# Block-sparse attention followed by a gated MLP: pair 6's transposes and the norm's pow moved ahead in their queues, three pairs' splits in other slots

## The chip, the cores and the metric

The kernel runs on one core of one Trainium2 chip. The metric is the device time of one execution in microseconds (us), the median of several runs. A core has five engines that run at once and wait for each other through semaphores: TensorE (PE, matrix products and transposes), VectorE (DVE), ScalarE (ACT), GpSimd (POOL) and SyncE (SP, which here issues nearly all DMAs). Every engine executes its own instructions strictly in program order, so an instruction that waits holds up all that stands behind it on its engine.

## The reference

Inputs are q, k, v of shape 4 x 8 x 768 x 64 (batch, head, position, dimension), and the weights of a gated MLP.

```python
scores = scale * np.matmul(q, k.transpose(0, 1, 3, 2))
scores = np.where(mask, scores, -1e9)      # mask by blocks of 32: window, edges, 3 sampled blocks
attn = softmax(scores)
x = np.matmul(attn, v)                     # heads side by side: 4 x 768 x 512
h = np.maximum(x @ w_in, 0.0)
u, v = h[..., :512], h[..., 512:]
v_n = (v - mean(v)) / np.sqrt(var(v) + 1e-06)
v_s = np.einsum('ts,bsd->btd', w_spatial, v_n) + b_spatial[None, :, None]
out = (u * v_s) @ w_out
```

## The kernel before

**Pairs.** Two heads make a pair p. There are 16 pairs, four to a batch element. For each head the kernel computes the scores by `qk_exp` (L361 on PE: two matmuls of 384 columns; L365 on ACT: the exponential), then the product with v by `av` (L377, six matmuls of 65 columns) and the division by the row sums by `norm` (L442 and L443 on DVE, writing `xn`). The first four pairs use versions for half of the columns: `qk_exp_half` (L396, L400), `av_half` (L412, L423, L424) and `xtr_half` (L433 on PE, L434 on DVE), which transposes `xn` into `xt`.

**How q and k get in.** `load(p)` issues three loads on SP (L110: q, k, v). `prepare(p)` casts k, q and v to bf16 on POOL (L140, L140, L143). `tr_dma(p, ...)` issues two DMA transposes on SP (L344, into `tt_k` and `tt_q`), each of which waits for its cast. `split_pair(p, "k")` and `split_pair(p, "q")` each issue two DVE copies (L350), one per head, from `tt_k` or `tt_q` into the operands `kt` and `qt` of the score matmuls. The first score matmul of a pair needs the first k copy and the first q copy.

**The order.** All instructions are issued in a hand-written order of slots; each slot holds one score step (a `qk_exp` or `qk_exp_half`), one AV step and one or two MLP steps. Slots are numbered g. The first loop has slots 0 to 47 (pairs 0 to 3); the second has 12 slots for each pair p from 4 on, g = 12p + s with s from 0 to 11. Within that loop p = NG is pair 4, and p = NP - 3 is pair 13. While pair p is computed, pair p + 1 is split, pair p + 2 is prepared and transposed, and pair p + 3 is loaded. `change` is true at pairs 8 and 12, where a new batch element begins.

**The MLP.** `moe_units(b)` returns a list of steps, one PE matmul of 512 columns each (L520), and these are popped slot by slot. A product into v goes through `v_post` (L533, L536, L537 on DVE: relu and statistics `mv`). After every third one, POOL computes `rstd` from the variance (L540 adds, L542 is the pow). `normalize` (L547 on DVE) needs `rstd` and writes `vn`, which the spatial products read (matmuls `vn,w_spt`); their results go through L586 on DVE to `gn` and by DMA transpose (L590) to `gt`, and the last products (`w_out_t,gt`) are stored from `osb` (L608, L610, L611). MLP products alternate between two PSUM banks, `moe0` and `moe1`; the third product from a given one reuses its bank. `xtr(p)` transposes `xn` by DMA (L466 on SP). `load_weights(2)` and `cast_weights(2)` bring in w_out (L175 on SP, L183 on POOL), as they do the other weights earlier.

Of the kernel before, what the change touches and what calls it, by code (L numbers as in the profile page):

```python
# [26 lines left out]
def kernel(  # L27
# [29 lines left out]
    NG = H // 2  # L57
    NP = B * NG
# [27 lines left out]
    def dram(src, b, h0, nh):  # L86
        return src[b, h0:h0 + nh].rearrange("h (p c) d -> p h (c d)", c=NCH)
# [13 lines left out]
    def st_tile(p, nm):  # L101
        if (nm, p) in st:
            return st[nm, p]
        st[nm, p] = work.tile([128, 2, NCH * D], FP32, tag=f"st_{nm}", bufs=2, name=f"st_{nm}")
        return st[nm, p]

    def load(p, names="qkv", eng=nc.sync):
        b, g = divmod(p, NG)
        for nm in names:
            eng.dma_start(out=st_tile(p, nm), in_=dram(dict(q=q, k=k, v=v)[nm], b, 2 * g, 2))  # L110
# [19 lines left out]
    def nat_tile(p, nm):  # L130
        nat[nm, p] = work.tile([128, NCH, 2, D], BF16, tag=f"nat_{nm}", bufs=2,
                               name=f"nat_{nm}")

    def cast_qk(p, nm, hs, eng):
        src = st[nm, p][:, hs].rearrange("p h (c d) -> p h c d", d=D)
        dst = nat[nm, p].rearrange("p c h d -> p h c d")[:, hs]
        if eng is nc.scalar:
            nc.scalar.activation(out=dst, in_=src, func=AF.Copy)
        else:
            eng.tensor_copy(out=dst, in_=src)  # L140

    def cast_v(p):
        nc.gpsimd.tensor_copy(  # L143
            out=vv[p % NG][:, :, :, 0:D],
            in_=st.pop(("v", p)).rearrange("p h (c d) -> p h c d", d=D))

    def prepare(p, names="kqv"):
        for nm in names:
            if nm == "v":
                cast_v(p)  # L150
            else:
                nat_tile(p, nm)
                cast_qk(p, nm, slice(0, 2), nc.gpsimd)
# [26 lines left out]
    def cast_weights(n):  # L180
        for _ in range(n):
            t, dst = w_staged.popleft()
            nc.gpsimd.tensor_copy(out=dst, in_=t)  # L183
# [26 lines left out]
    def keep_warm(n):  # L210
        for _ in range(n):
            nc.tensor.matmul(out=wps[:, 0:128], lhsT=warm, rhs=warm, start=True, stop=True)  # L212
# [51 lines left out]
    def qt_mask(h0, h1, grp, eng=nc.vector):  # L264
        cols = slice(grp * HALF, (grp + 1) * HALF)
        eng.tensor_copy(out=qt_all[D:KR, h0:h1, cols],
                              in_=qt_all[D:KR, 0:1, cols].to_broadcast([NB, h1 - h0, HALF]))
# [17 lines left out]
    def bank(shape, dtype):  # L285
        moe_bank[0] = 1 - moe_bank[0]
        return psum.tile(shape, dtype, tag=f"moe{moe_bank[0]}", bufs=1, name="ps_moe")
# [40 lines left out]
    def mask_product(hf, ps, copy):  # L328
        mq = ps[0:NB, 0:HALF]
        nc.tensor.matmul(out=mq, lhsT=bm, rhs=ind[:, hf * HALF:(hf + 1) * HALF],  # L330
                         start=True, stop=True)
        copy(qt[0][D:KR, hf * HALF:(hf + 1) * HALF], mq)
# [14 lines left out]
    def split_pair(p, nm):  # L347
        src = tt.pop((nm, p)).rearrange("x c n -> x (c n)")
        for h in range(2):
            nc.vector.tensor_copy(out=(qt if nm == "q" else kt)[(2 * p + h) % H][0:D, :],  # L350
                                  in_=src[h * D:(h + 1) * D, :])
# [34 lines left out]
    def qk_exp_half(g):  # L386
        gh, i = divmod(g, NCH // 2)
        grp, j = divmod(gh, H)
        if g % NCH == 0:
            t = work.tile([128, NCH, S], BF16, tag="a_all", bufs=3, name="a_all")  # L390
            t = t.rearrange("p c s -> p (c s)").rearrange("p (u c s) -> p u c s", u=2, c=NCH)
            a_ref["half", gh], a_ref["half", gh + 1] = t[:, 0], t[:, 1]
        ps = psum.tile([128, 1024], FP32, tag="sc", bufs=2)
        for u in range(2):
            ci = 2 * i + u
            nc.tensor.matmul(out=ps[:, u * 512:u * 512 + HALF],  # L396
                             lhsT=kt[j][:, ci * 128:(ci + 1) * 128],
                             rhs=qt[j][:, grp * HALF:(grp + 1) * HALF],
                             start=True, stop=True)
        nc.scalar.activation(out=a_ref["half", gh][:, 2 * i:2 * i + 2, :],  # L400
                             in_=ps.rearrange("p (b c) -> p b c", b=2)[:, :, 0:HALF],
                             func=AF.Exp, scale=0.125)
# [223 lines left out]
    def cast_q_pair(p, half):  # L626
        cast_q(p, half, slice(0, 2), nc.gpsimd)
# [44 lines left out]
    for g in range(N0):  # L672
        qk_exp_half(g)
        if g < 6:
            keep_warm(2)
        if g == 12:
            mask_product(1, bank([128, 512], FP32), dve_copy)
        if g == 0:
            qt_mask(1, 2, 0)
        if g == 1:  # L680
            tr_k_head(1, 0, NCH)
            cast_qk(1, "k", slice(0, 1), nc.vector)
            qt_mask(2, 4, 0)
        for p, third in tr_slots.get(g, ()):
            tr_pair(p, "k", third)
        if g in q_slots:
            tr_q_pair(*q_slots[g])
        if g == 13:
            for p in range(2):
                cast_q_pair(p, 1)  # L690
            qt_mask(4, 8, 1, nc.gpsimd)
            cast_q_pair(2, 1)
            cast_weights(2)
            cast_q_pair(3, 1)
            cast_weights(2)
            prepare(4, "kq")
            load_weights(3)
        if g in (6, 20):
            qt_mask(*{6: (4, 8, 0), 20: (1, 4, 1)}[g])
        if g == 26:  # L700
            moe_q.extend(moe_units(0))
        if g == 28:
            tr_dma(4, "k")
            tr_dma(4, "q")
            cast_weights(2)
            load(4, "v")
            load(5, "kqv")
            wspt(0)
            wspt(1)
            cast_weights(1)  # L710
            prepare(5, "kq")
            wspt(2)
            wspt(3)
            tr_dma(5, "k")
            tr_dma(5, "q")
            wspt(4)
            wspt(5)
            load(6)
        if g in (36, 42):
            cast_v(4 if g == 36 else 5)  # L720
        if g in (39, 45):
            split_pair(4, "k" if g == 39 else "q")
        first_batch_rest(g)
        if g >= 26 and g != 32:
            moe_q.popleft()()
        first_batch_x(g)

    for p in range(NG, NP + 1):
        for s in range(12):
            g = 12 * p + s  # L730
            change = NG < p < NP and p % NG == 0
            j, ci = divmod(g, NCH)
            if p == NP and g - LAG >= 2 * NP * NCH:
                break
            if p < NP:
                qk_exp(j, ci)
            if p + 1 < NP and s in ((3, 6) if p == NG else (7, 10)):
                split_pair(p + 1, "k" if s in (3, 7) else "q")
            if s == (10 if p == NG else 8 if change else 6) and p + 2 < NP:
                tr_dma(p + 2, "k")  # L740
                tr_dma(p + 2, "q")
            if s == (7 if p == NG else 1) and p + 2 < NP:
                prepare(p + 2)
                if p == 6:
                    cast_weights(2)
            if s == (9 if change else 7) and p + 2 < NP:
                if p + 3 < NP:
                    load(p + 3)
                if p == 5:
                    load_weights(2)  # L750
            if g < N0 + 11 and g != N0 + 8:
                moe_q.popleft()()
            if g == N0 + 11:
                slots_left = 49
            if moe_q and slots_left > 0:
                budget += len(moe_q) / slots_left
                slots_left -= 1
                while moe_q and budget >= 0.5:
                    moe_q.popleft()()
                    budget -= 1  # L760
            first_batch_rest(g)
            first_batch_x(g)
            if g >= N0 + LAG:
                ja, qc = divmod(g - LAG, NCH)
                av(ja, qc)
                if qc == NCH - 1:
                    norm(ja)
            if s == (6 if change else 8) and p > NG:
                xtr(p - 1)
            if s == 11 and change:  # L770
                moe_q.extend(moe_units(p // NG - 1))
                slots_left = 48 if p < NP - NG else 49
                budget = 0.0
# [34 lines left out]
```

## Time and profile before

| | us |
|---|---|
| median of 6 runs | 217.43 |
| lowest and highest of them | 216.46 and 218.79 |
| the profiled execution's own time | 217.39 |
| its span, first to last instruction | 215.6 |
| PE busy in the span | 207.5 |
| ACT, DVE, POOL busy | 172.3, 132.6, 69.5 |

The profile shows one execution. In the timeline each row has the start from the span's beginning, the duration, the engine, the source line, the operation with what it writes and reads, and how many like it are merged; in square brackets stands the time for which the engine sat idle before it and what ended the wait. Rows of one engine may overlap a little, since its instructions are pipelined. A DMA row on SPq is the issue alone; the transfer lands later. PE's granted clock is full throughout (1.00 in the windows of all stages but the last, 0.99 there).

### The profile page before, as it was taken

To read this page: it belongs to the slowest core of one execution; us is meant where nothing else is said; L and a number is where in the kernel's file an instruction comes from. 1 tells how busy PE (TensorE), PEld (TensorE's weight loads), DVE (VectorE), ACT (ScalarE), POOL (GpSimd) and SP (SyncE) were. 2 spreads that over 40 slices of the span, in tenths; PEclk is the share of its full clock that TensorE was granted. 3 is DMA by queue.
4 is the path that set the end of the run, shared out by engine and by line. 5 is a ranking of instruction groups with operands and counts; after the bars stand their busy time and mean duration, and the time that the engine had idled before them with its cause. 6 is when DMAs were issued, how large, how long until landed. Compare 5 with 4: busy or idle time off the path is not lost.

```text
span 215.6 us, 5268 instructions
## 1 busy us (share of the span) xinstructions
PE 207.5 (96%) x2099; PEld 125.3 (58%) x2099; DVE 132.6 (61%) x311; ACT 172.3 (80%) x238; POOL 69.5 (32%) x97
## 2 busy tenths in 40 slices
PE   8999999899979999999999999999999999999993
PEld 6667766466646666655556566555555655544441
DVE  7877759967554745356958464455978444585542
ACT  7999999799978999998899888888889885266031
POOL 6877979702626140403242400401502000022000
PEclk9999999999999999999999999999999999999999
DMA  6999999988999798999979348999712124620246
GB/s 167 312 354 392 395 289 228 253 150 278 250 253 263 146 256 171 262 288 315 186 190 255 58 83 246 222 194 298 119 30 40 24 52 87 220 101 0 59 119 236
DMA packets 64936, 42.24 MB, mean 196 GB/s; under 512 B 46896, under 2 KB 60560, under 8 KB 64912
## 3 DMA queue, kind: packets, MB, share of 16 engines
q1 hardware_dynamic: 64624, 41.58, 76.4%
q8 instruction: 16, 0.26, 0.5%
q10 hardware_dynamic: 288, 0.33, 0.5%
q14 instruction: 8, 0.07, 0.2%
HBM read 24.38 MB, written 6.29 MB: 142 GB/s over the span
## 4 chain that ended last, share of the span: by engine, by line
PE 86%; DVE 9%; issue 1%; POOL 1%; DMA 1%; ACT 1%; ACTq 0%; DVEq 0%; POOLq 0%
PE ps_moe L520 34%; PE ps L361 20%; PE ps_av L377 12%; PE ps L396 6%; PE ps_av L412 4%; PE ps_t L520 3%; PE ps_sc L520 3%; DVE kt_all L350 2%; DVE vsb L533 2%; PE wps L212 2%; DMA out_dram<-osb 1%; DVE kt_all L277 1%; DVE osb L610 1%; PE ps_av L433 1%; PE ps_moe L322 1%
## 5 line engine op out<-in xcount | busy, mean ns | idle before, releaser
L365 ACT ACTIVATE a_all<-ps 128x768 bf16<-128x768 f32 x144 | 113.4, 813 | 16.0 <-PE ps L361 9.6
L361 PE MATMUL ps<-qt_all,kt_all 88*128 88x384 bf16 x288 | 70.3, 325 | 1.2 <-DVE qt_all L350 1.2
L377 PEld LDWEIGHTS <-a_all 128*128 128x128 bf16 x864 | 46.1, 97 | 34.0 <-issue 1.6
L377 PE MATMUL ps_av<-vv,a_all 128*128 128x65 bf16 x864 | 50.8, 194 | 0.0
L520 PE MATMUL ps_moe<-w_in_t,xt 128*128 128x512 bf16 x160 | 50.0, 378 | 0.7 <-DVE vsb L533 0.4
L400 ACT ACTIVATE a_all<-ps 128x768 bf16<-128x768 f32 x48 | 35.6, 812 | 2.6 <-PE ps L396 2.2
L520 PE MATMUL ps_moe<-vn,w_spt 128*128 128x512 bf16 x120 | 35.6, 378 | 0.0
L140 POOL CAST nat_k<-st_k 128x768 bf16<-128x768 f32 (+1 forms) x14 | 10.9, 779 | 73.6 <-DMA st_k<-in_k_dram 56.1
L586 DVE SCALAR_TENSOR_TENSOR gn<-ps_moe,b_col,un 128x512 bf16<-128x512 f32 x20 | 15.0, 749 | 20.7 <-PE ps_moe L520 20.5
L520 PEld LDWEIGHTS <-xt 128*128 128x128 bf16 x192 | 18.6, 97 | 15.0 <-issue 0.7
L396 PE MATMUL ps<-qt_all,kt_all 88*128 88x384 bf16 x96 | 23.4, 325 | 0.5 <-ACT a_all L400 0.2
L520 PE MATMUL ps_moe<-w_out_t,gt 128*128 128x512 bf16 x80 | 23.0, 378 | 0.0
L520 PEld LDWEIGHTS <-w_spt 128*128 128x128 bf16 x144 | 13.8, 97 | 11.6
L361 PEld LDWEIGHTS <-kt_all 88*128 88x128 bf16 x288 | 19.0, 98 | 1.8 <-DVE qt_all L350 1.3
L412 PEld LDWEIGHTS <-a_all 128*128 128x128 bf16 x288 | 14.9, 98 | 6.3 <-issue 0.9
L533 DVE TENSOR_SCALAR vsb<-ps_moe 128x512 bf16<-128x512 f32 x18 | 12.3, 682 | 10.1 <-PE ps_moe L520 10.0
L536 DVE BATCH_NORM_STATS2 stats<-vsb 128x6 f32<-128x512 bf16 x24 | 16.7, 694 | 1.5 <-ACT vsb L531 0.9
L412 PE MATMUL ps_av<-vv,a_all 128*128 128x65 bf16 x288 | 17.0, 194 | 0.4 <-DVE xt L434 0.4
L540 POOL TENSOR_SCALAR std<-mv 128x3 f32<-128x3 f32 x8 | 1.9, 242 | 42.9 <-DVE mv L537 30.6
L610 DVE COPY osb<-ps_moe 128x512 f32<-128x512 f32 x10 | 6.9, 690 | 13.3 <-PE ps_moe L520 13.2
L443 DVE TENSOR_TENSOR xn<-ps_av,rc 128x384 bf16<-128x384 f32 x24 | 13.4, 557 | 0.8
L520 PEld LDWEIGHTS <-gt 128*128 128x128 bf16 x96 | 8.8, 97 | 7.2
(100 smaller groups left out, 212.9 us busy)
## 6 DMA issues: line engine op xcount, KB each, us to landing
out_dram<-osb SPq DMA_DIRECT2D x23, 256.0 KB, 3.0
st_v<-in_v_dram SPq DMA_DIRECT2D x14, 384.0 KB, 5.5
st_k<-in_k_dram SPq DMA_DIRECT2D x13, 384.0 KB, 4.4
st_q<-in_q_dram SPq DMA_DIRECT2D x12, 384.0 KB, 3.6
wst<-in_moe_w_spatial_dram SPq DMA_DIRECT2D x3, 768.0 KB, 9.1
wst<-in_moe_w_in_dram SPq DMA_DIRECT2D x4, 512.0 KB, 8.0
wst<-in_moe_w_out_dram SPq DMA_DIRECT2D x2, 512.0 KB, 6.4
st_q<-in_q_dram SPq DMA_DIRECT2D x4, 192.0 KB, 6.2
```

Source lines behind the costliest of these rows:

```text
L140: eng.tensor_copy(out=dst, in_=src)
L361: nc.tensor.matmul(out=ps[:, hf * 512:hf * 512 + HALF], lhsT=kt[j % H][:, ci * 128:(ci + 1) * 128], rhs=qt[j % H][:, hf * HALF:(hf + 1) * ...
L365: nc.scalar.activation(out=a_ref[j][:, ci, :].rearrange("p (b c) -> p b c", b=2), in_=ps.rearrange("p (b c) -> p b c", b=2)[:, :, 0:HALF], ...
L377: nc.tensor.matmul(out=av_ref[j][:, qc, :], lhsT=a_ref[j][:, ci, qc * 128:(qc + 1) * 128], rhs=vv[p % NG][:, h, ci, :], start=(ci == 0), s ...
L396: nc.tensor.matmul(out=ps[:, u * 512:u * 512 + HALF], lhsT=kt[j][:, ci * 128:(ci + 1) * 128], rhs=qt[j][:, grp * HALF:(grp + 1) * HALF], s ...
L400: nc.scalar.activation(out=a_ref["half", gh][:, 2 * i:2 * i + 2, :], in_=ps.rearrange("p (b c) -> p b c", b=2)[:, :, 0:HALF], func=AF.Exp, ...
L412: nc.tensor.matmul(out=av_ref["half", gh][:, qc, :], lhsT=a_ref["half", gh][:, ci, qc * 128:(qc + 1) * 128], rhs=vv[p][:, h, ci, :], start ...
L443: nc.vector.tensor_tensor(out=xn_ref[p][:, :, h, :], in0=ps[:, :, 0:D], in1=rc.to_broadcast([128, NCH, D]), op=ALU.mult)
L520: nc.tensor.matmul(out=box[0], lhsT=lhs, rhs=rhs, start=(i == 0), stop=(i == n - 1))
L533: nc.vector.tensor_scalar(out=vsb[:, tcc, :], in0=ps, scalar1=0.0, scalar2=None, op0=ALU.max)
L536: nc.vector.bn_stats(out=stats, in_=vsb[:, tcc, :])
L586: nc.vector.scalar_tensor_tensor(out=gn[:, tcc, :], in0=ps, scalar=b_col[:, tcc:tcc + 1], in1=un[:, tcc, :], op0=ALU.add, op1=ALU.mult)
```

## The change

- First loop: pair 4's k split goes from slot 39 to slot 44, its q split from 45 to 46.
- p = 4: `tr_dma(6)` stays at s = 10; `load(7)` goes from s = 7 to s = 11. On SP the order of pair 6's two transposes and pair 7's three loads is thus exchanged.
- p = 5: pair 6's splits go from s = 7 and 10 to s = 6 and 8; `prepare(7)` from s = 1 to 7; `tr_dma(7)` from 6 to 9; `load(8)` and the loads of w_out from 7 to 10. On POOL, L540 and L542 now stand ahead of pair 7's three casts; on SP the transpose of pair 4's `xn` (L466) now stands ahead of pair 7's transposes.
- p = 13: pair 14's splits go from s = 7 and 10 to s = 5 and 6.

Nothing is added or removed; PE and ACT have the same instructions in the same order.

```diff
-        if g in (39, 45):
-            split_pair(4, "k" if g == 39 else "q")
+        if g in (44, 46):
+            split_pair(4, "k" if g == 44 else "q")
...
     for p in range(NG, NP + 1):
+        change = NG < p < NP and p % NG == 0
+        splits = {NG: (3, 6), NG + 1: (6, 8), NP - 3: (5, 6)}.get(p, (7, 10))
+        s_prep = {NG: 7, NG + 1: 7}.get(p, 1)
+        s_tr = {NG: 10, NG + 1: 9}.get(p, 8 if change else 6)
+        s_load = {NG: 11, NG + 1: 10}.get(p, 9 if change else 7)
         for s in range(12):
...
-            if p + 1 < NP and s in ((3, 6) if p == NG else (7, 10)):
-                split_pair(p + 1, "k" if s in (3, 7) else "q")
-            if s == (10 if p == NG else 8 if change else 6) and p + 2 < NP:
+            if p + 1 < NP and s in splits:
+                split_pair(p + 1, "k" if s == splits[0] else "q")
+            if s == s_prep and p + 2 < NP:
+                prepare(p + 2)
+                if p == NG + 2:
+                    cast_weights(2)
+            if s == s_tr and p + 2 < NP:
                 tr_dma(p + 2, "k")
                 tr_dma(p + 2, "q")
-            if s == (7 if p == NG else 1) and p + 2 < NP:
-                prepare(p + 2)
-                if p == 6:
-                    cast_weights(2)
-            if s == (9 if change else 7) and p + 2 < NP:
-                if p + 3 < NP:
-                    load(p + 3)
-                if p == 5:
+            if s == s_load and p + 3 < NP:
+                load(p + 3)
+                if p == NG + 1:
                     load_weights(2)
```

More of the change, by code (lines that the diff above doesn't have):

```diff
@@ L728 @@
     for p in range(NG, NP + 1):
+        change = NG < p < NP and p % NG == 0
[3 more added lines that the diff above has]
+        s_load = {NG: 11, NG + 1: 10}.get(p, 9 if change else 7)
         for s in range(12):
             g = 12 * p + s
-            change = NG < p < NP and p % NG == 0
             j, ci = divmod(g, NCH)
```

## The prediction

> **What bounds the kernel now.** I read the page first, then PE's timeline for its idle stretches, then the engines that end them.
>
> ```profile
> PE 207.5 (96%) x2099; PEld 125.3 (58%) x2099; DVE 132.6 (61%) x311; ACT 172.3 (80%) x238; POOL 69.5 (32%) x97
> ```
> PE sets the time: it is idle for 215.6 - 207.5 = 8.1 us, mostly at the start (1.4 us in the first 20) and the end (4.1 us in the last 26). Between these, its timeline has four idle stretches:
> ```profile
> 39.02 0.34 PE L433 MATMUL ps_av<-ident,xn 128*128 128x128 bf16 x3 [0.69 <-DVE xn L424]
> ...
> 40.80 0.35 PE L412 MATMUL ps_av<-vv,a_all 128*128 128x65 bf16 x6 [0.38 <-DVE xt L434]
> ...
> 63.59 0.50 PE L361 MATMUL ps<-qt_all,kt_all 88*128 88x384 bf16 x2 [1.21 <-DVE qt_all L350]
> ...
> 153.66 0.59 PE L520 MATMUL ps_moe<-w_in_t,xt 128*128 128x512 bf16 x2 [0.45 <-DVE vsb L533]
> ```
> Their sum, 0.69 + 0.38 + 1.21 + 0.45 = 2.73 us, is all that an exchange of order can win here; PE's work stays. Each ends with DVE. DVE's timeline at the three places:
> ```profile
> 35.53 2.95 DVE L350 COPY kt_all<-tt_k 64x768 bf16<-64x768 bf16 x2
> 38.61 0.36 DVE L424 TENSOR_TENSOR xn<-ps_av,rc 128x192 bf16<-128x192 f32 x1
> 41.15 1.33 DVE L350 COPY qt_all<-tt_q 64x768 bf16<-64x768 bf16 x2
> ...
> 57.67 0.18 DVE L537 BATCH_NORM_AGGREGATE mv<-stats 128x2 f32<-128x6 f32 x1
> 60.77 0.41 DVE L547 TENSOR_SCALAR vn<-vsb,mv,rstd 128x512 bf16<-128x512 bf16 x1 [2.92 <-POOL rstd L542]
> 61.80 0.73 DVE L350 COPY kt_all<-tt_k 64x768 bf16<-64x768 bf16 x2
> 62.54 0.73 DVE L547 TENSOR_SCALAR vn<-vsb,mv,rstd 128x512 bf16<-128x512 bf16 x2
> 63.19 0.73 DVE L350 COPY qt_all<-tt_q 64x768 bf16<-64x768 bf16 x2
> ...
> 151.51 1.50 DVE L350 COPY kt_all<-tt_k 64x768 bf16<-64x768 bf16 x2
> 152.94 0.67 DVE L533 TENSOR_SCALAR vsb<-ps_moe 128x512 bf16<-128x512 f32 x1
> ```
> The same two copies take 0.73 us at 61.80, but 2.95, 1.33 and 1.50 elsewhere. POOL's timeline tells why:
> ```profile
> 38.36 0.83 POOL L140 CAST nat_k<-st_k 128x768 bf16<-128x768 f32 x1 [0.46 <-DMA st_k<-in_k_dram]
> 39.77 0.83 POOL L140 CAST nat_q<-st_q 128x768 bf16<-128x768 f32 x1 [0.58 <-PE ps L396]
> 40.54 1.73 POOL L143 CAST vv<-st_v 128x768 bf16<-128x768 f32 x2
> ...
> 58.62 0.83 POOL L143 CAST vv<-st_v 128x768 bf16<-128x768 f32 x1 [0.35 <-PE ps L361]
> 59.53 0.23 POOL L540 TENSOR_SCALAR std<-mv 128x3 f32<-128x3 f32 x1
> 59.85 0.89 POOL L542 TENSOR_TENSOR rstd<-std,mhalf 128x3 f32<-128x3 f32 x1
> ...
> 150.31 0.83 POOL L140 CAST nat_k<-st_k 128x768 bf16<-128x768 f32 x1 [13.18 <-DMA st_k<-in_k_dram]
> 151.08 0.83 POOL L140 CAST nat_q<-st_q 128x768 bf16<-128x768 f32 x1
> 151.85 0.95 POOL L143 CAST vv<-st_v 128x768 bf16<-128x768 f32 x1
> ```
> Taken singly, a copy alone lasts 0.34 to 0.36 us. One that meets a running cast ends 0.21 us after the cast's row ends: 38.11 after 37.90 (a w_spatial cast), 42.47 after 42.26, 153.01 after 152.80. And between two copies a waiting cast gets in first. Each meeting costs a copy up to 0.8 us.
>
> **The change, part by part.** All is set against the profiled 217.39 us.
>
> *Pair 4 (g = 44, 46).* The k copies leave 35.53, so L424 no longer waits behind them: its AV product is ready at 36.65, and xn by 37.2. The transposes of slot 43 start when PE gets there, 0.69 earlier. L533 then starts after its product ends (37.60), and L434 at 37.64 + 1.54 = 39.18 (the 1.54 is the distance of the two rows before, 38.88 to 40.42). It ends at 39.5, PE wants its bank at 40.80 - 0.38 - 0.69 = 39.73: the 0.38 goes too. Up to 1.07 us are free. What is late next are the copies themselves. The first k copy runs from 39.42 to 39.76; POOL's nat_q cast comes at 39.77 (its row names a matmul, but what it overwrites was read long before: I take its load for what ended the wait), a tie. If the second k copy goes first, L423 and L424 end by 40.75, the first q copy meets the vv cast and ends at 41.58, and slot 48's score matmul, due at 42.68 - 1.07 = 41.61, hardly waits. If the cast goes first, the k copy ends at 40.80, xn at 41.39, the q copy stands behind the second vv cast until about 42.35, and the matmul comes at 42.40: 0.28 is left of 1.07. If nat_q's load lands 0.35 earlier, both k copies are caught, and slot 48 comes about 0.3 later than before. There is also a lid: pair 5's k copies wait for `tt_k`, landed at 46.42 by a chain of DMAs that PE does not set; L423 stands behind them, so xn of slot 53 is not ready before 47.14 + 0.57 = 47.7 and slot 55's transposes (48.45 before) not before 47.77: at most 0.68. Bounds -0.3 and +0.68; I take 0.45, about the middle of the two likelier outcomes, 0.28 and 0.68.
>
> *Pair 6 and the pow (p = 5).* L537 ends at 57.85; L540 and L542 now follow on POOL, which has nothing ahead of them since pair 6's v cast (ends 54.9): rstd at 57.85 + 0.3 + 0.9 = 59.05 instead of 60.74. On DVE the k copies go first (57.9 to 58.6), then one L547 (59.1), L442, L443 (to 60.3: its AV step was issued before 58.3), then q (60.3 to 61.0), then two L547. Slot 72's matmul is due at 63.59 - 1.21 = 62.38, so there is a reserve of 1.4 us even for one cast in the way (0.8). Behind it, PE waits for the last two vn at about 62.9 and 63.7; they are ready by 61.8, or 62.6 with a cast. The k copies need `tt_k` of pair 6. Its transposes stay at 53.36 and 54.67, for they wait for casts; before, `tt_q` landed at 59.97, after pair 7's v load (58.49), which was issued ahead of it. Now only pair 6's loads are ahead (last landed 53.80), and the row for a free queue (tt_k of pair 8: issued 70.74, landed 73.53, 2.8 us) gives 56.2 and 57.5. Gain 1.21, of which I count 1.20 (0.05 us lies between copy and matmul); low bound 0.9, if a late `tt_k` takes part of the reserve.
>
> *What pays for it: pair 7's chain.* Its loads go from 49.51 to behind the transposes, about 56.1 (q), 56.7, 57.2; with 4.0 and 5.5 us to landing, as pair 8's had, k is there at 60.7 and v at 62.7. Its casts run from 60.7 to 63.5, so the pow delays none of them. The xn transpose of pair 4 is ahead on SP, ready at 60.3, gone by 61.6; then tt_k at 61.7, tt_q at 63.0, landing by 66. Pair 8's loads go from 60.11 to 64.3, w_out's to 65.9, the first gt transpose from 66.23 to 66.9, and from there SP is held by gn (69.45) as before, so the queue has caught up. Cover: pair 7's k split is at about 69, its q split is needed at 73.95 - 1.65 = 72.3; w_out, cast by about 74 instead of 71.9, is first read at 81.98 - 1.65 = 80.3. All this costs nothing unless a landing slips by over 5 us. Beside pair 7's k copies POOL now casts pair 8 instead of w_out, so they take about 1.5 us, as 1.57 before.
>
> *Pair 14 (p = 13).* Before, the k copies (1.50) held L533 to 152.94 and PE lost 0.45. Now all four copies start after L537 (149.77): k to 150.40, but POOL's nat_k comes at 150.31 and the first q copy waits for it, to about 151.4; nat_q goes in between, the second ends at 152.3; then L442, L443, and L533 at about 153.0, as before. If the load lands 0.5 later, the copies are through and L533 starts at 151.9: +0.45. If 0.3 earlier, one more copy is caught: -0.85. I take 0: here the change only trades one meeting for others.
>
> [...]
>
> **Sum.** 0.45 + 1.20 + 0 = 1.65; 217.39 - 1.65 = 215.74. The median of before is 0.04 above its profiled run: 215.8.
>
> **The rivals.**
> *Everything goes through* (both ties fall to DVE): 0.68 + 1.21 + 0.45 = 2.34, 215.1. For it: casts depend on DMA landings, which may fall either way. Against: all four pairs of copies that ran beside casts before (35.5, 41.1, 70.5, 151.5) met one.
> [...]
> *The stall at slot 72 stays*: DVE now stands at pair 6's k copies ahead of L547. If `tt_k` lands at L, slot 72 comes at L + 2.2 (k 0.73, then L547 0.33, L442 0.22, L443 0.48, q 0.40, by the distances of the rows). It is as late as before at L = 61.4; the slowest transpose in these stages (8.8 us, issued at 62.84, landed at 71.62) would make it 62.1. Then about 0.5 is lost against before, and pair 4's 0.45 makes up for it: 217.4. Against: the queue ahead is empty.
> *Slower: pair 7 arrives too late.* With the slowest landings of the rows in a chain (9.1 us, the w_spatial loads; 8.8 us, the transpose), k is there at 65.8, tt_q is issued at 67.5 and lands at 76.3, and slot 84 comes at 76.7 instead of 72.3: 4.4 - 1.65 = 2.7 slower, 220.1. It decides from a landing of tt_q beyond 71.9, and makes the kernel measurably slower beyond 71.9 + 1.65 + 1.1 = 74.7. For it: the DMA queue is near full (share 0.91 to 1.21 from 54 to 80). Against: those slow rows had up to five loads ahead of them, and here there is one transpose.
>
> **How the numbers follow.** Chances: the forecast 0.52, everything through 0.15, the port 0.17, the stall stays 0.06, pair 7 late 0.10. About 0.5% (1.09 us, 216.34) is what a measurement can tell from no change. Faster: 0.52 + 0.15, less 0.05 for the forecast's upper tail, plus 0.02 of the port's lower end, 0.64. Slower 0.10. The rest, 0.26, is the same. The range runs from 214.9 (all through, less 0.2 for the spread of medians) to 217.4 (the port's case and the stall's), and leaves out the late pair 7 and a little of each side.
>
> **What would show it.** PE without idle before slot 72's L361 and the L547 row at about 59 right after L542 show the second part; L424 at about 36.9 the first, with the end of pair 4's q copy against slot 48. For pair 14, look at when nat_k starts against the four copies. I am wrong if PE idles at 72 or 84 for want of qt, or if L533 of pair 13 begins after 153.5 less the shift.

## The result and the profile after

The change makes the kernel slower: 219.89 us (median of 21 runs, 218.11 to 224.29) against 217.56 (median of 47 in the same sessions). The ratio to the kernel before is 1.010, 95% interval 1.0079 to 1.0121. The forecast was 215.8 in a range of 214.9 to 217.4. The comparison leaves out executions more than 1.5% above the fastest of their own kernel, so the ratio need not be the quotient of the medians.

The ratio mixes two costs, which the mean granted clock of each execution separates. One stretch of 3.41 us at half speed, as in the profile below, makes it 0.992 over a span of 216 us; I call such a stretch a drop. Of the 26 executions of the changed kernel, the 4 of its second profile's session included, 22 have 0.992 or less; of the 82 of the kernel before whose clock is on record (from the sessions of the experiments), 32 have. Without a drop the changed kernel takes 218.5 us (median of 4) and the kernel before 217.5 (median of 50). So about 1 us seems to be lost at full clock too, and the clock drops in most executions instead of in two of five. No profile of the kernel before caught a drop in mid-kernel; which wait brings it there is not known.

The profiled execution of the changed kernel took 221.27 us, its span is 219.5. Its distance from the trace before can be read slot by slot, by the start of each slot's first score matmul:

| up to slot | after minus before, us | what happened since |
|---|---|---|
| 4 | +2.34 | PE's clock came late (below); not the change |
| 46 | +1.10 | pair 4's part: 1.24 won |
| 72 | -0.10 | pair 6's part: 1.20 won |
| 104 | -0.11 | nothing |
| 108 | +3.94 | 4.05 lost |
| 188 | +3.84 | nothing |

So both gains came, and a larger loss stands in slot 105 (the expectations below call it 107). PE's timeline of the changed kernel, with its idle stretches after the start:

```profile
94.96 0.39 PE L520 MATMUL ps_moe<-w_out_t,gt 128*128 128x512 bf16 x1 [2.38 <-DMA gt<-gn]
...
157.51 0.59 PE L520 MATMUL ps_moe<-w_in_t,xt 128*128 128x512 bf16 x2 [0.43 <-DVE vsb L533]
```
The stretches at slots 43, 45 and 72 are gone; a new one of 2.38 us waits for a DMA: the sixth transpose from `gn` to `gt` of batch element 0. The chain of waits over this stretch leads back to its issue:

```profile
88.53 6.39 DMA gt<-gn
```
Its input, gn, was ready at 82.36, so the transfer waited 6.2 us for its turn. SP's timeline shows what stood ahead of it. First the changed kernel:

```profile
65.43 0.57 SPq L110 DMA_DIRECT2D st_q<-in_q_dram  x1
...
69.07 3.04 SPq L590 DMA_TRANSPOSE gt<-gn  x2
73.14 1.77 SPq L344 DMA_TRANSPOSE tt_k<-nat_k  x1
75.00 1.24 SPq L344 DMA_TRANSPOSE tt_q<-nat_q  x1
76.30 0.57 SPq L110 DMA_DIRECT2D st_q<-in_q_dram  x1
...
84.20 1.24 SPq L344 DMA_TRANSPOSE tt_k<-nat_k  x1
...
86.83 0.57 SPq L110 DMA_DIRECT2D st_q<-in_q_dram  x1
...
88.53 1.25 SPq L590 DMA_TRANSPOSE gt<-gn  x1
```
and the same stations before, where this gt transpose was issued at 85.53:

```profile
60.11 0.57 SPq L110 DMA_DIRECT2D st_q<-in_q_dram  x1
...
66.23 4.42 SPq L590 DMA_TRANSPOSE gt<-gn  x2
70.74 1.24 SPq L344 DMA_TRANSPOSE tt_k<-nat_k  x1
...
73.38 0.57 SPq L110 DMA_DIRECT2D st_q<-in_q_dram  x1
...
81.22 1.24 SPq L344 DMA_TRANSPOSE tt_k<-nat_k  x1
...
83.84 0.57 SPq L110 DMA_DIRECT2D st_q<-in_q_dram  x1
...
85.53 1.19 SPq L590 DMA_TRANSPOSE gt<-gn  x1
```
Pair 8's loads are 5.3 us later (65.43 against 60.11). From pair 9's loads on, the rows shown are 2.9 to 3.0 later: 76.30 against 73.38, 84.20 against 81.22, 86.83 against 83.84, and gt 88.53 against 85.53. Besides, the transfer now takes 6.39 us to landing instead of 4.61; pair 10's v load, issued ahead of it, lands at 94.45, just before it. Together gt lands at 94.91 instead of 90.14. PE would have used it at 92.58 now; before, its first use was the second matmul of this row, at 92.54, so 2.4 us were to spare:

```profile
92.32 0.59 PE L520 MATMUL ps_moe<-w_out_t,gt 128*128 128x512 bf16 x2
```

The other 1.67 us of the 4.05 I put down to the clock; the run "The wait filled with work" below tests this. In the windows of this stretch the columns are the busy time (and instructions) of each engine, PEclk, DMA share and GB/s:

```profile
92.00:95.00 3.00, 0.62 (x6) 0.14 (x3) 0.94 (x3) 1.70 (x3) 1.60 (x3) 1.00 1.62 125
95.00:98.00 3.00, 3.00 (x20) 1.60 (x21) 0.00 (x0) 1.19 (x2) 0.77 (x1) 0.57 1.08 383
98.00:101.00 3.00, 3.00 (x31) 1.75 (x29) 1.45 (x3) 2.05 (x3) 0.00 (x0) 0.86 1.15 281
```
From 95.42 to 98.83 PE was granted half speed, right after the wait. Half speed for 3.41 us leaves 1.71 us of work undone.

DVE's timeline at the three places of the change:

```profile
39.23 0.36 DVE L424 TENSOR_TENSOR xn<-ps_av,rc 128x192 bf16<-128x192 f32 x1
...
41.77 0.73 DVE L350 COPY kt_all<-tt_k 64x768 bf16<-64x768 bf16 x2
42.90 0.73 DVE L350 COPY qt_all<-tt_q 64x768 bf16<-64x768 bf16 x2
...
58.87 0.71 DVE L350 COPY kt_all<-tt_k 64x768 bf16<-64x768 bf16 x2
60.36 0.41 DVE L547 TENSOR_SCALAR vn<-vsb,mv,rstd 128x512 bf16<-128x512 bf16 x1 [0.78 <-POOL rstd L542]
61.38 1.24 DVE L350 COPY qt_all<-tt_q 64x768 bf16<-64x768 bf16 x2
...
154.25 1.92 DVE L350 COPY qt_all<-tt_q 64x768 bf16<-64x768 bf16 x2
156.78 0.68 DVE L533 TENSOR_SCALAR vsb<-ps_moe 128x512 bf16<-128x512 f32 x1
```
and POOL beside it:

```profile
59.37 0.96 POOL L542 TENSOR_TENSOR rstd<-std,mhalf 128x3 f32<-128x3 f32 x1
61.49 0.92 POOL L140 CAST nat_k<-st_k 128x768 bf16<-128x768 f32 x1 [1.17 <-DMA st_k<-in_k_dram]
...
154.23 0.83 POOL L140 CAST nat_k<-st_k 128x768 bf16<-128x768 f32 x1 [12.59 <-DMA st_k<-in_k_dram]
155.00 0.95 POOL L140 CAST nat_q<-st_q 128x768 bf16<-128x768 f32 x1
```
Pair 4's copies run in 0.73 each, free of casts in this execution. The pow ends before pair 7's casts begin, and the first q copy of pair 6 is through before slot 72. At pair 14 the q copies now meet two casts (1.92), and L533 is as late as before.

### The profile page after: what moved, and what is told of

Same layout as the page of the kernel before. It is cut to its first block, busy times and chain, and to the rows that moved or that the text cites. A ratio compares the mean times of both kernels' runs of the same rounds, so it can differ in the third digit from the quotient of the medians.

```text
span 219.5 us, 5267 instructions
## 1 busy us (share of the span) xinstructions
PE 211.3 (96%) x2099; PEld 127.3 (58%) x2099; DVE 132.5 (60%) x311; ACT 172.7 (79%) x238; POOL 69.8 (32%) x97
## 4 chain that ended last, share of the span: by engine, by line
PE 49%; DVE 4%; DMA 4%; SPq 2%; issue 1%; ACT 0%; ACTq 0%; DVEq 0%
PE ps_moe L520 24%; PE ps L361 12%; PE ps_av L377 8%; DMA gt<-gn 3%; PE ps_t L520 3%; PE ps_sc L520 3%; DVE vsb L533 1%; DMA out_dram<-osb 1%; DVE qt_all L350 1%; SPq L344 1%; SPq L110 1%; DVE stats L536 1%; DVE gn L586 0%; DVE osb L610 0%; ACT osb L608 0%
## 5 line engine op out<-in xcount | busy, mean ns | idle before, releaser
L361 PE MATMUL ps<-qt_all,kt_all 88*128 88x384 bf16 x288 | 71.1, 328 | 0.0
L520 PE MATMUL ps_moe<-w_out_t,gt 128*128 128x512 bf16 x80 | 23.9, 388 | 2.4 <-DMA gt<-gn 2.4
L396 PE MATMUL ps<-qt_all,kt_all 88*128 88x384 bf16 x96 | 24.7, 340 | 0.4 <-ACT a_all L400 0.2
L533 DVE TENSOR_SCALAR vsb<-ps_moe 128x512 bf16<-128x512 f32 x18 | 12.3, 684 | 10.9 <-PE ps_moe L520 10.8
L540 POOL TENSOR_SCALAR std<-mv 128x3 f32<-128x3 f32 x8 | 2.0, 247 | 48.1 <-DVE mv L537 34.1
```

What stands on the lines that cost most here:

```text
L361: nc.tensor.matmul(out=ps[:, hf * 512:hf * 512 + HALF], lhsT=kt[j % H][:, ci * 128:(ci + 1) * 128], rhs=qt[j % H][:, hf * HALF:(hf + 1) * ...
L396: nc.tensor.matmul(out=ps[:, u * 512:u * 512 + HALF], lhsT=kt[j][:, ci * 128:(ci + 1) * 128], rhs=qt[j][:, grp * HALF:(grp + 1) * HALF], s ...
L520: nc.tensor.matmul(out=box[0], lhsT=lhs, rhs=rhs, start=(i == 0), stop=(i == n - 1))
L533: nc.vector.tensor_scalar(out=vsb[:, tcc, :], in0=ps, scalar1=0.0, scalar2=None, op0=ALU.max)
```

## The experiments

Three theories stood against each other. **The queue**: the moves at pairs 4 and 5 made SP's in-order queue run late, and the transfer with the least to spare pays. **The transfers**: the DMA engines are full in this stage (their share is 1.02 and 1.10 in the windows from 84 to 92 and 92 to 95 us of the trace before) and set a fixed time, whatever the order. **The start or the splits**: the loss is not in the queue at all. All ratios are to the kernel before, run on the same chip, with 95% intervals.

**gt ahead of pair 10's loads** (to the changed kernel):

```diff
-s_load = {NG: 11, NG + 1: 10}.get(p, 9 if change else 7)
+s_load = {NG: 11, NG + 1: 10, NG + 3: 9}.get(p, 9 if change else 7)
```


> The changed kernel with one exchange on SP: in pair 7's slots the three loads of pair 10 go from s = 7 to s = 9, behind the sixth gt transpose of batch 0 and the xn transpose of pair 6. Theory (the SP queue): the changed kernel lost 2.38 us of PE time at slot 107 because that gt transpose stood behind pair 10's loads, which were issued 3 us later than before, and about 1.7 us more because PE's granted clock fell to half after the idle stretch. With the exchange gt is issued at about 86.8 instead of 88.5, lands by about 89 instead of 94.9, PE is not idle there, no drop of the clock: 4.05 us less than the changed kernel, about 215.3 (before 217.4 less 1.23 at slots 43 to 46 and 1.21 at slot 72, plus up to 0.4). Rival (the transfers themselves are slow in this stage, whatever their order): gt still lands after 92.6, and the time stays at 218.5 to 219.7. Second rival (the loss is in the start, where the profiled run was 2.34 us late by slot 4): 219 to 221.

Measured: 1.0103 (1.006 to 1.0146), no gain. Yet in its profile gt was issued at 86.47, landed at 89.77, and PE passed slot 105 without a wait: slot 108 is at 92.87, 1.76 us ahead of before. The loss appears one place on, in PE's timeline of this kernel:

```profile
99.68 0.61 PE L520 MATMUL ps_moe<-w_in_t,xt 128*128 128x512 bf16 x1 [3.78 <-DMA xt<-xn]
```
Pair 10's loads, another 3 us later (89.84), and four stores stand right ahead of pair 7's xn transpose (issued at 94.06). PE waited 3.78 us for it and was at half clock for about 6.8 (PEclk 0.50 in the windows from 98 to 104, 0.81 from 104 to 106). The expected 215.3 was wrong. The new stall fits the first theory, though it was not forecast: the lateness went on to the next transfer that PE needs soon.

**The old queues with the new splits** (to the changed kernel):

```diff
-s_prep = {NG: 7, NG + 1: 7}.get(p, 1)
-s_tr = {NG: 10, NG + 1: 9}.get(p, 8 if change else 6)
-s_load = {NG: 11, NG + 1: 10}.get(p, 9 if change else 7)
+s_prep = {NG: 7}.get(p, 1)
+s_tr = {NG: 10}.get(p, 8 if change else 6)
+s_load = 9 if change else 7
```


> The changed kernel's splits (pairs 4, 6 and 14) with the loads, casts and transposes of pairs 6 to 8 where the kernel before had them; the order on SP and POOL is that of the kernel before. Theory (the SP queue): no wait for gt, so no loss at slot 107. The stall at slot 72 shrinks, since pair 6's k copies are ahead of the vn step and only one vn step, the division and the q copy follow the pow: q is ready at about 62.2 on the clock of the trace before, whatever PE does, because the pow waits for casts that DMA landings time. PE, 1.1 us earlier from pair 4, would want it at 61.3: stall of 0.9 instead of 1.21; net gain about 1.4, 216.0. Rival (the queues' order is what removes the stall at slot 72): the stall grows to 1.2 + 1.1, net 0, 217.4. Second rival (the splits, not the queues, cost the time at slot 107): 218.5 or more.

Measured: 0.9991 (0.9961 to 1.0021), the same as before. With the order on SP and POOL put back, the loss at slot 105 is gone, so it belongs to the queues and not to the splits; a granted clock of 0.992 or less is in 1 of its 12 executions. The second half of the expectation failed: the stall at slot 72 did not shrink from 1.21 to 0.9 but was 1.65.

```profile
63.37 0.50 PE L361 MATMUL ps<-qt_all,kt_all 88*128 88x384 bf16 x2 [1.65 <-DVE qt_all L350]
```

**Pair 4's splits alone** (to the kernel before), run twice:

```diff
-if g in (39, 45):
-    split_pair(4, "k" if g == 39 else "q")
+if g in (44, 46):
+    split_pair(4, "k" if g == 44 else "q")
```


> The kernel before with pair 4's two splits in slots 44 and 46 and nothing else. If the casts that time the pow at slot 72 follow DMA landings and not PE, the 1.1 us won at slots 43 to 46 are given back at slot 72 (its stall grows from 1.21 to about 2.3) and the time is 217.4. If the stall at slot 72 moves with PE, 216.3.

> Pair 4's splits alone once more, with more rounds, since its three timed runs were 219.5 to 220.7 and its profiled one 217.7. If PE's 1.1 us are handed back at slot 72 and nothing else happens: 217.4, the same as before. If a PE that is even a little earlier meets a late gt transpose in most runs: 218.5 to 219.5.

Measured: 1.012 (1.0074 to 1.0165) with four runs, then 1.0006 (0.9961 to 1.0051) with twelve. I take the second. The three timed runs of the first all have a granted clock of 0.992, so one drop each; of the twelve, three have. At the rate of the kernel before (32 of 82), three in a row would come by chance once in 17 times. In both profiles 1.24 us are won at slots 43 to 46. In the first, 0.44 is given back by slot 49, and slot 72 waits longer than in the first trace of the kernel before:

```profile
63.38 0.50 PE L361 MATMUL ps<-qt_all,kt_all 88*128 88x384 bf16 x2 [1.34 <-DVE qt_all L350]
```
In the second it waits for 1.27. So only 0.06 to 0.13 of the gain is handed back there, not the 1.1 that was expected. Yet the times do not show the rest: without a drop the nine others of the twelve take 217.5 us in the median, as the kernel before does in that session. The gain is counted against one trace, and the stalls that it removes vary (see "Why the prediction was wrong").

**The new queues with the old splits** (to the changed kernel):

```diff
-if g in (44, 46):
-    split_pair(4, "k" if g == 44 else "q")
+if g in (39, 45):
+    split_pair(4, "k" if g == 39 else "q")
...
-splits = {NG: (3, 6), NG + 1: (6, 8), NP - 3: (5, 6)}.get(p, (7, 10))
+splits = {NG: (3, 6)}.get(p, (7, 10))
```


> The kernel before with the change's loads, casts and transposes of pairs 6 to 8 (SP and POOL as in the changed kernel), and all splits where the kernel before had them. Theory (the SP queue): stall at slot 72 gone (1.2 us gained), the sixth gt transpose again behind pair 10's loads and landing at about 94.9; PE wants it at 94.96 - 2.38 + 1.1 = 93.7, so a stall of about 1.2 with or without a drop of the clock: 217.4 to 219. If the queues are innocent: 216.2.

Measured: 1.0049 (1.001 to 1.0088), slower, with both stalls in PE's timeline. Its eight executions without a drop take 218.75 us in the median, those of the kernel before in the same session 217.58, so about 1.2 us are lost there without any drop:

```profile
63.82 0.50 PE L361 MATMUL ps<-qt_all,kt_all 88*128 88x384 bf16 x2 [1.27 <-DVE qt_all L350]
...
94.31 0.39 PE L520 MATMUL ps_moe<-w_out_t,gt 128*128 128x512 bf16 x1 [1.38 <-DMA gt<-gn]
```
The wait for gt is there as the queue theory has it, without a drop of the clock. That the stall at slot 72 would vanish was wrong: the pow was early (L547 at 59.34 instead of 60.77), but the two other L547 (1.75 for both) and the q copies (1.36) then met pair 7's casts. Here the pow's move pays only together with the splits'.

**Pair 8's loads early** (to the changed kernel):

```diff
-s_load = {NG: 11, NG + 1: 10}.get(p, 9 if change else 7)
+s_load = {NG: 11, NG + 1: 8}.get(p, 9 if change else 7)
...
-                if p == NG + 1:
-                    load_weights(2)
+            if p == NG + 1 and s == 10:
+                load_weights(2)
```


> The changed kernel with pair 8's three loads at s = 8 of pair 5, ahead of pair 7's transposes on SP instead of behind them (w_out's loads stay at s = 10). Theory (lateness handed down the SP queue): the 3 us by which every later load and transpose ran late began here, since pair 8's loads waited on SP for pair 7's transposes, these for pair 7's casts, and these for pair 7's late loads. With the exchange pair 8's loads go at about 59 to 60 again, the sixth gt transpose at about 85.5 as before, landing at 90 to 91; PE wants it at 92.54 - 2.4 = 90.1, so a stall below 1 us and no drop of the clock: 215 to 216.5 (before 217.4). Rival (any shift in front hits a fixed time of the transfers, so what PE wins is handed back): gt lands at 92 or later whatever the order, stall 2 or more, 217.4 to 219.5.

Measured: 0.9959 (0.991 to 1.0008). The 1.0% that the change cost is gone, and with it the drops: 1 of 12 executions has one. Without a drop this kernel is no faster than the one before (217.9 against 217.5 us in the median). Pair 9's loads are issued at 73.70 and pair 10's at 84.75 (before 73.38 and 83.84, changed 76.30 and 86.83): the lateness began where the theory puts it. But gt lands at 92.58, not at 90 to 91, while PE is 1.45 us ahead of before:

```profile
92.63 0.39 PE L520 MATMUL ps_moe<-w_out_t,gt 128*128 128x512 bf16 x1 [1.38 <-DMA gt<-gn]
```
gt was issued at 86.46, 0.93 later than before, and took 6.13 us to landing instead of 4.61. So the rival holds for a part: even with the queue nearly punctual, PE wins here only as much as gt has to spare.

**The wait filled with work** (to the changed kernel): ten matmuls without use ahead of the product that waits, into the bank that it overwrites. `filled` is 10 for the sixth `w_out_t,gt` product of batch element 0, and 0 elsewhere.

```diff
+                if i == 0 and filled:
+                    for _ in range(filled):
+                        nc.tensor.matmul(out=box[0], lhsT=warm, rhs=w_in_t[:, 0, 0:512],
+                                         start=True, stop=True)
```


> The changed kernel with ten matmuls of 512 columns without use in front of the sixth out product of batch 0, into the PSUM bank which that product then overwrites: work of 2.16 us in the place where PE waited 2.38 us for gt. It leaves the transfers as they are. Theory (the loss of 4.05 us at slot 107 is 2.38 of waiting and 1.67 of half clock that the idle stretch brings): PE is idle there for 0.2 to 0.5 us only, the granted clock stays at full, and the kernel is 1.7 us faster than the changed one: 218.0 (changed one 219.7). Rival (the clock's drop has another cause, or the loss is all waiting): 219.7 as the changed one, or 221.8 if the matmuls come on top.

Measured: 1.0013 (0.9978 to 1.0048); the changed kernel had 1.010. None of its 12 executions shows a drop in mid-kernel (granted clock 0.997 or more), against 22 of 26 of the changed kernel. PE's timeline of it:

```profile
91.23 2.32 PE L521 MATMUL ps_moe<-w_in_t,warm 128*128 128x512 bf16 x10
93.41 0.39 PE L524 MATMUL ps_moe<-w_out_t,gt 128*128 128x512 bf16 x1
```
No idle time, the granted clock stays at 1.00, and between slots 104 and 108 this kernel loses 2.18 us against before, not 4.05. So more work in the same place wins 1.87 us in the profile, about the 1.71 of the half clock. It saves the drop, not the wait: without a drop this kernel takes 218.9 us in the median, no less than the changed one's 218.5.

**Pair 14 in free stretches of DVE**, on top of pair 8's loads early:

```diff
-splits = {NG: (3, 6), NG + 1: (6, 8), NP - 3: (5, 6)}.get(p, (7, 10))
+splits = {NG: (3, 6), NG + 1: (6, 8), NP - 3: (1, 5)}.get(p, (7, 10))
```


> The kernel with pair 8's loads early, and in it pair 14's splits at s = 1 and s = 5 instead of 5 and 6: k goes into the free stretch of DVE after the division of slot 156, q after the second statistics, ahead of pair 15's casts on POOL. If what delays L533 there is the meeting of the copies with the casts, L533 follows its product, PE has no stall in that pair (0.43 in the changed kernel) and the time is 0.4 to 0.5 below that of the kernel with the loads early. If the copies are late by themselves, no difference.

Measured: 1.0003 (0.9957 to 1.0049), not below the one before. The local step did what was expected: no stall at pair 13, and 0.60 us won between slots 164 and 168. What hid it in the profile is gt again: 1.63 us of waiting at slot 105. In the times, 7 of its 12 executions have a drop, against 1 of 12 of the one before; why so many is open.

**And pair 10's v load behind gt**, on top of both:

```diff
-                load(p + 3)
+                load(p + 3, "qk" if p == NG + 3 else "qkv")
+            if p == NG + 3 and s == 9:
+                load(p + 3, "v")
```


> As the one before (loads of pair 8 early, pair 14's splits at s = 1 and 5), and pair 10's v load goes behind the sixth gt transpose on SP (s = 9 of pair 7). One load of 384 KB less stands ahead of gt: it lands 1.0 to 1.5 us earlier, which takes the rest of the stall at slot 107. Expected 0.3 to 1.0 below the one before, about 215; if gt is no longer late there, no difference.

Measured: 0.9945 (0.991 to 0.9981), the only version here that is faster than the kernel before beyond its interval. gt lands at 91.87 and PE waits 0.10 us. Against the kernel of the step before, gt lands 1.45 us earlier, as expected, but hardly because it landed faster (5.69 us from issue instead of 5.87). It was issued 1.27 earlier, and 0.75 of that is in the queue ahead of this edit (pair 10's q load at 85.00 instead of 85.75). One of the 12 executions has a drop. Pair 14's q copies now run from 149.11 and L533 at 150.94 follows its product.

**These two edits alone on the kernel before**:

> The kernel before with two edits alone: pair 14's splits at s = 1 and 5 of pair 13, and pair 10's v load behind the sixth gt transpose (s = 9 of pair 7). Nothing of the change in front of slot 72. If the version with pair 8's loads early owes its time to these two edits alone, this one is as fast: 216.2. If the moves at pairs 4 and 6 count in it (1.2 to 1.4 us of PE time at slot 72, then partly lost to gt), this one gains only the 0.45 of pair 14: 217.0.

Measured: 0.999 (0.9951 to 1.0029). Its profile has no stall at pair 13, but 1.58 us at slot 72. In the profiles the moves at pairs 4 and 6 thus count in the faster version: counted from slot 4, it ends 1.65 us ahead of the first trace, this one 0.83. The times cannot tell: the two intervals overlap, and without a drop both versions take 217.08 us in the median, of 11 and of 9 executions.

**Second profiles of the two kernels**:

> The kernel before once more, for a second profile of the stage around slot 107. If the 2.4 us between the landing of the sixth gt transpose (90.14) and its first use (92.54) belong to the kernel, they are seen again. If the landing wanders by 1 to 3 us from run to run, as in the kernels that keep the old queue (91.9 and 92.8 there), the margin is smaller or gone here.

> The changed kernel once more, for a second profile. By the SP queue theory PE waits again for gt at slot 107, 2 to 2.5 us, with a drop of the clock after it, and slot 4 is not 2.3 us late, since nothing in front of slot 39 was changed: span 217 to 217.5 instead of 219.5. If the late start belongs to the change, it is there again.

The kernel before took 219.57 us in this one execution. PE's timeline:

```profile
65.61 0.50 PE L361 MATMUL ps<-qt_all,kt_all 88*128 88x384 bf16 x2 [2.75 <-DVE qt_all L350]
...
94.92 0.39 PE L520 MATMUL ps_moe<-w_out_t,gt 128*128 128x512 bf16 x1 [0.20 <-DVE qt_all L350]
```
Pair 7's casts began at 59.09 here instead of 56.66, so slot 72 waited 2.75 us instead of 1.21, and gt landed at 94.88 with nothing to spare (the second row names a DVE copy, but the landing is 0.04 ahead of it). Both numbers of the first trace were one draw of a value that wanders with the landings. The changed kernel had 1.0111 (1.0032 to 1.0189) and, in its profile,

```profile
95.48 0.39 PE L520 MATMUL ps_moe<-w_out_t,gt 128*128 128x512 bf16 x1 [4.15 <-DMA gt<-gn]
```
with slot 4 only 0.21 us later than in the trace before. The late start is thus not the change's. gt landed at 95.43 here, PE came 1.25 us earlier, the wait is 4.15 us, and half clock follows again. (The expected span of 217 to 217.5 was too low for that reason: 220.6.)

## Why the prediction was wrong

**Pair 4** won more than the 0.45 of the sum when it is counted against the first trace: 1.24 at the slots themselves, and 0.53 to 1.24 after what was given back by slot 56, in the ten profiles with these splits. The tie with nat_q's cast did not decide it. In the changed kernel's profile the late start had carried the copies past the casts; in others up to 0.7 was lost at slot 48, as worked out, but never the whole. But the first trace was a high draw: the stalls before slots 43 and 45 are 1.07 there and 0.42, 0.52 and 0.78 in the three other profiles with the old splits.

**Pair 6 and the pow** won 1.20 in the changed kernel's two profiles, the figure of the sum, by the steps named: mv, pow, L547, division, q copy. The queues' part in it was real too: without it (old queues) the stall stays at 1.65, with it but without the new splits at 1.27.

**Pair 14** gave nothing, as forecast, and by the meeting described: the first q copy ends 0.21 us after nat_k's row (155.27 after 155.06). The stall was 0.43, and 1.03 in the second profile, inside the bounds. As in the trace before, a copy that meets a cast ends 0.21 us behind it, less than a whole copy takes (0.32 to 0.36). No run shows "the port" of the chances and of the range, nor what holds a copy back. What the runs show are meetings of copies with casts: pair 4's copies had none in the changed kernel's first profile (0.73 for each two), pair 14's q copies had two (1.92).

**The step that failed is pair 7's chain**, in two sentences of the prediction.

The first is "from there SP is held by gn (69.45) as before, so the queue has caught up". It had not. Pair 8's loads were issued at 65.43 (forecast 64.3), and the two gt transposes behind them at 69.07 and 70.38, so the pause in which SP had waited for gn was used up. k took 6.0 us to landing where the trace before had 4.0, its cast came at 72.16, and pair 8's transpose was issued at 73.14 instead of 70.74. In the second profile k took only 3.9, but transposes took up to 2.8 us to issue, and pair 9's loads were 3.4 late all the same. From there SP issues each entry right behind the one before it, in both kernels, so nothing could be made up: up to gt the entries stay 2.9 to 3.9 later.

The second is "All this costs nothing unless a landing slips by over 5 us": the cover was worked out for pair 7's q split and for w_out, but not for the last transfers of the same queue. The sixth gt transpose had 2.4 us to spare (90.14 to 92.54), and the gain in the sum itself was to move PE 1.65 toward it. 3.0 of lateness plus 1.65 exceeds 2.4 by 2.2 even without a slower transfer: this could have been read from the trace before, from rows that the prediction does not use. The rival "pair 7 arrives too late" named the right side and the right resource, but the wrong place: pair 7's q landed at 68.47, in time. The signs of being wrong that it named did not show the loss either: in the changed kernel's first profile PE idled neither at slot 72 nor at 84, and L533 of pair 13 came as late as before.

The third omission is the clock. A wait was priced at its length; here a wait of 2.38 us cost 4.05.

Two slips in the working decided nothing. The 4.1 us of idleness at the end were read from a window that runs 0.4 us past the span; it is 3.7. And in the rival "the stall at slot 72 stays", a landing at 62.1 is 0.7 and not 0.5 behind the 61.4 that it is set against, so that its time would be 217.6.

## What to carry to other kernels

Where one in-order queue carries loads, transposes and stores, price a moved transfer at the last consumer of that queue, not at the nearest one: list for every later entry when it landed and when it was first needed, and take off both the lateness that is added and the time that the compute engine is meant to win. Here a gain in front of such a queue was worth only the smallest of those margins. Moving the transfer with the least to spare ahead was not enough, for the lateness went on to the next one; issuing the loads earlier at which the lateness began did help. And read margins from more than one trace, and the granted clock of every execution: here a margin of 2.4 us was 0 in the next trace, and the clock dropped in 32 of 82 executions of one kernel and in 22 of 26 of the other.

## What the runs showed of the hardware

**Half clock came after waits of 2.4 us and more, but not after every one.** In the changed kernel's first profile the clock is full from 10.08 to 95.42 us and half from there to 98.83, for 3.413. The 85.33 us of full clock are 25 times these 3.413. From 98.83 to the next fall at 218.30, where PE runs out of work, it is 35 times, and in the first profile of the kernel before (3.83 to 215.46) 62 times. In the last 3.41 us ahead of these three falls PE was idle for 2.38, 2.48 and 3.41. In the second profile of the changed kernel half clock lasts from about 96.1 to 99.5, after a wait of 4.15 of which 2.8 lie in the 3.41 us ahead of the fall; in the kernel with gt ahead it lasts from about 97.9 to 104.8, and the 3.41 us ahead hold 2.0 of its 3.78. No drop came after 2.75 us at slot 72 in the second profile of the kernel before (granted clock 1.00 over the run), nor after 1.38 at slot 105 in the new queues with the old splits and with pair 8's loads early. So the length of a wait alone does not decide. From these multiples and idle times I estimate that the clock is set in steps of 3.41 us: counted from full clock at about 6.4 us in that profile (from the lengths of its first matmuls), the 2.75 fall into two steps with about 1.6 and 1.1. How much idleness in a step it takes is not shown: 2.0 us, in the kernel with gt ahead, is the least before a fall here. The idle times rest on modelled ends of matmuls.

**The late start is the clock as well.** Full clock was granted at 10.08 us in the first profile of the changed kernel, at 3.83 in that of the kernel before and, by the lengths of the first matmuls, at about 4.0 in the second of the changed one. In the first, the score matmuls took 0.53 us each until then instead of 0.33, and slot 4 came at 10.54 instead of 8.20 and 8.42. The instructions up to slot 38 are the same. So the clock is not quite full throughout in the trace before: the warm-up matmuls (`wps<-warm`) take 0.31 us each before 3.83 us and 0.22 behind it, and the windows print 1.00 for both.

**In most profiles the transpose landed right behind the transfer that was issued ahead of it.** In ten of the twelve where both landings are known, the sixth gt transpose landed 0.46 to 0.54 us after the transfer ahead of it; in the two others (the old queues with the new splits, and the second of the kernel before) 1.83 and 1.93. Its own time to landing was 3.3 us behind two other transposes (gt ahead of pair 10's loads), 4.1 to 6.4 behind three loads. It did not simply grow with the number of loads: behind two of them, the two kernels with pair 10's v load moved behind it have 4.2 and 5.7.
